# A packed-attention and MLP kernel: the next batch's first scores put right behind a weight fold, into another pair of PSUM banks, and the first residual put in front of the second scores

## The chip, the cores and the metric

The kernel runs on 1 core of a Trainium2 chip. The metric is the device time of one execution in microseconds (us). Before the change the median of 3 runs is 764.5 us (764.04 to 764.6). The engines are named as in the profile: PE is the matrix engine, PEld its weight load, DVE the vector engine, ACT the scalar engine, POOL the general engine, SP the queue that issues DMA transfers.

## The reference

Inputs are q, k, v of shape (8 batches, 8 heads, 576 tokens, 64), packs p of shape (8, 8, 32, 64), and the mixer's weights U (576 x 32), V (32 x 576), w_ch1 (512 x 2048), w_ch2 (2048 x 512). All is float32.

```python
def sm_attn(qq, kk, vv):
    s = scale * np.matmul(qq, kk.transpose(0, 1, 3, 2))
    s = s - np.max(s, axis=-1, keepdims=True)
    a = np.exp(s)
    a = a / (np.sum(a, axis=-1, keepdims=True) + 1e-09)
    return np.matmul(a, vv)
p_packed = sm_attn(p, k, v)
out = sm_attn(q, p_packed, p_packed)      # 576 tokens against 32 packs a head
# x = out with its heads side by side, (8, 576, 512)
h = x.transpose(0, 2, 1) @ U @ V
u = x + h.transpose(0, 2, 1)
result = u + np.maximum(u @ w_ch1, 0.0) @ w_ch2
```

## The kernel before, in words

The kernel never forms x. A batch's attention weights `a` (8 heads x 32 packs = 256 rows, 576 tokens) are mixed over the tokens with U and V, and u @ w_ch1 is computed as `a` times a folded weight, packs @ w_ch1. Products that need full float32 are split into a high and a low part and take three matmuls.

From batch 2 on, the program works on batch b while it prepares the attention of batch b+1 and the folded weights that come next. The order of the work is written out by hand: the string `batch_steps` is run once for each of the batches 2 to 7, and each word in it calls the next piece of one kind of work. All instructions of an engine run in the order in which the words issue them; an engine that waits at one instruction holds all behind it. What differs from batch to batch is only the tile that a word works on. In the last batch the words for the next batch's attention do nothing, so those run five times (during batches 2 to 6).

The words that this document needs, with the lines of the profile:

- **H** is half of a first-product tile (PE, L100 to L102, six matmuls of 320 or 256 columns) into one of two PSUM banks called `h_ps`, tag "k". **E** (ACT, L1034) and **L** (ACT, L801) apply the relu and empty that bank.
- **U** builds sums of such tiles (DVE, L1046, L1047, L1048), **C** splits off their high parts (ACT, L1069) and **D** their low parts (DVE, L1074). C and D write the tiles `h`.
- **G** is one turn of the second product (PE, L1085, 3 or 6 matmuls into the banks `o`). It reads what C and D wrote; the third matmul of a column's first turn is the first that reads D's part.
- **F0** folds a quarter of w_ch1 (PE, L562, into two banks `t_ps`, tag "t"; four such quarters a batch, the weights in one tile `w1s` that a DMA fills). **F1** (ACT, L574) copies the high part out, **F2** (DVE, L576) the low part, four each. F1 and F2 on one bank take turns: the third F1 waits for the first F2, the fourth for the second.
- **q0, q1, q2** transpose q (PE, L301 and L304, banks of tag "t"); q0a to q2a copy it out (L310, L312).
- **s3** makes the scores of four heads (PE, L321, into two banks); the first s3 of a batch is that of group 0, the second of group 1. **s4** transposes them out of the banks (DVE, L363, twice), **s5** takes the maximum (DVE, L367), **s6** subtracts it (POOL, L371), **s7** is the exponential (ACT, L374), **s8** the sum, the small constant and the reciprocal (DVE, L379, L381, L383; D stands between the second and the third), **s9** the product (POOL, L371), **sa** the transpose back (DVE, L387).
- **t1** transposes both groups' weights (PE, L327 and L329).
- **A** adds the residual u for half the tokens, 32 small products (PE, L1114).

PSUM has two banks of tag "t", two of tag "k" and four of `o`. A tile of a tag takes the bank that its tag's tile before last had, and waits until that is read.

The products of L562 and L321 use 64 rows and 32 columns of the PE array at a time (in the profile 64\*32), those of L1114 32 rows and 64 columns (32\*64), and all others here the whole (128\*128).

Of the kernel before, what the change touches and what calls it, by code (L numbers as in the profile page):

```python
# [20 lines left out]
def packed_attention_mixer_kernel(  # L21
# [28 lines left out]
    B, H, S, D = q.shape  # L50
    NP = p.shape[2]
    R = U.shape[1]
    DM = H * D
    DF = w1.shape[1]
    P = 128
# [15 lines left out]
    U, V, w1, w2 = (a.bitcast(I32) for a in (U, V, w1, w2))  # L71
# [37 lines left out]
    def bank():  # L109
        return psT.tile([P, 512], F32, name="t_ps", tag="t")  # L110
# [203 lines left out]
    def scores(lT, t, g, ss):  # L314

        for x in range(4):
            hs, h = slice(32 * x, 32 * x + 32), x ^ g
            for r in range(2):
                rs = slice(64 * r, 64 * r + 64)
                n = HALF[r].stop - HALF[r].start  # L320
                nc.tensor.matmul(ss[r][hs, :n], lhsT=lT[rs, g, hs], rhs=t[rs, h, :n], start=True, stop=True)  # L321
# [10 lines left out]
    def attention(b, res):  # L332

        st = {}
# [18 lines left out]
            turned(st["t", g], st["t_ps", g, h], h, scalar)  # L353

        def scores_q(g):
            ss = st["ss", g] = [bank() for _ in range(2)]
            scores(ppT[b], st["t", g], g, ss)

        def side(g, r):
# [97 lines left out]
        if b != 2:  # L457
            gh = list(product(range(2), range(2)))
            return {
                "a0": [load], "a1": [run(load_q, 1)],  # L460
                **{f"q{h}": [run(turn_q, g, h) for g in range(2)] for h in range(3)},
                **{f"q{h}a": [lambda scalar, g=g, h=h: turned_q(g, h, scalar) for g in range(2)] for h in range(3)},
                "s3": [run(scores_q, g) for g in range(2)],
                "s4": [run(side, g, r) for g, r in gh],
                "s5": [run(most, g) for g in range(2)],
                "s6": [run(each, g, "m", ALU.subtract) for g in range(2)],
                "s7": [run(power, g) for g in range(2)],
                "s8": [run(total, g, k) for g in range(2) for k in range(3)],
                "s9": [run(each, g, "s", ALU.mult) for g in range(2)],
                "sa": [run(back, g) for g in range(2)],  # L470
                "t0": [room],
                "t1": [run(tokens, k) for k in (0, 2, 4)],
                "t2": [run(split_tokens, k, False) for k in (0, 2, 4)],
                "t3": [run(split_tokens, k, True) for k in (0, 2, 4)],
                "x0": [mix1], "x1": [run(split_mix1, False)], "x2": [run(split_mix1, True)],
                "y0": [run(mix2, g, hf) for hf, g in gh],
                "y1": [run(add_mix2, g, hf) for hf, g in gh],
                "y2": [run(high_mix2, g, hf) for hf, g in gh],
                "y3": [run(low_mix2, g, hf) for hf, g in gh],
                "pu": [put],  # L480
            }
# [5 lines left out]
        def step_scores(g):  # L487
            scores_q(g)
            side(g, 0)
            side(g, 1)  # L490
# [102 lines left out]
    for z in range(2):  # L593
        a, b = (x[:, D:].rearrange("p (y z n) -> p z y n", y=2, z=2) for x in (swapped, ident))
# [665 lines left out]
    for kt in range(NK):  # L1260
# [41 lines left out]
        "Sn F2n F1n Pn Hn F1n U XO XM F1n XO F2n En F2n En XM F2n Wn Zn XO XO Yn "  # L1302
    )
    batch_steps = (
# [9 lines left out]
    )  # L1314
    joint_steps = (
# [123 lines left out]
```

## Time and profile before

| | |
|---|---|
| median of 3 runs | 764.5 us |
| the profiled execution, and its span | 765.2 us, 763.2 us |
| PE busy | 749.9 us, 98% |
| DVE, ACT, POOL busy | 587.5, 405.7, 84.9 us |
| granted TensorE clock | 1.000 |
| DMA | 151.78 MB, 199 GB/s |

In the timeline a row gives the start in us from the span's beginning, the duration of what is merged into the row, the engine, the line, what is written and read, the shape and the count; idle time before it and what ended it stand in brackets. The products of F0 and s3 stand twice in the trace. Matmuls overlap in time, so the distance between two starts says what one cost the engine, and the printed duration does not.

### The profile page before, as it was taken

To read this page: it belongs to the slowest core of one execution; us is meant where nothing else is said; L and a number is where in the kernel's file an instruction comes from. 1 tells how busy PE (TensorE), PEld (TensorE's weight loads), DVE (VectorE), ACT (ScalarE), POOL (GpSimd) and SP (SyncE) were. 2 spreads that over 40 slices of the span, in tenths; PEclk is the share of its full clock that TensorE was granted. 3 is DMA by queue.
4 is the path that set the end of the run, shared out by engine and by line. 5 is a ranking of instruction groups with operands and counts; after the bars stand their busy time and mean duration, and the time that the engine had idled before them with its cause. 6 is when DMAs were issued, how large, how long until landed. Compare 5 with 4: busy or idle time off the path is not lost.

```text
span 763.2 us, 19553 instructions
## 1 busy us (share of the span) xinstructions
PE 749.9 (98%) x7795; PEld 662.2 (87%) x7795; DVE 587.5 (77%) x1216; ACT 405.7 (53%) x1018; POOL 84.9 (11%) x116
## 2 busy tenths in 40 slices
PE   8999999999999999999999999999999999999997
PEld 6667787887878889998999989999999989999997
DVE  4799789976787768867888768867887678764876
ACT  4788765554343645555455544555554554555451
POOL 1123111010111002100201002010201020200000
PEclk9999999999999999999999999999999999999999
DMA  9999984369112874656478474657464746463672
GB/s 318 337 355 305 324 219 157 112 228 300 40 42 88 254 250 140 221 195 200 130 229 267 132 245 148 185 168 244 145 192 166 253 126 202 148 239 125 198 224 105
DMA packets 106090, 151.78 MB, mean 199 GB/s; under 512 B 40464, under 2 KB 60176, under 8 KB 102416
## 3 DMA queue, kind: packets, MB, share of 16 engines
q1 hardware_dynamic: 105856, 150.28, 61.6%
q8 instruction: 62, 1.02, 0.5%
q14 instruction: 28, 0.23, 0.1%
q10 hardware_dynamic: 144, 0.26, 0.1%
HBM read 116.56 MB, written 33.95 MB: 197 GB/s over the span
## 4 chain that ended last, share of the span: by engine, by line
PE 85%; DMA 6%; DVE 4%; ACT 3%; issue 1%; SPq 0%; POOL 0%; ACTq 0%
PE o L1085 33%; PE h_ps L100 9%; PE h_ps L101 8%; PE h_ps L102 8%; PE t_ps L562 4%; PE o L100 3%; PE o L101 3%; PE o L102 3%; DMA w1s<-w1D 2%; DMA kx<-in_k_dram 2%; PE t_ps L301 1%; PE o L1114 1%; PE s_ps L321 1%; PE t_ps L321 1%; PE m_ps L696 1%
## 5 line engine op out<-in xcount | busy, mean ns | idle before, releaser
L1085 PE MATMUL o<-w2h,h 128*128 128x256 f32 x832 | 166.9, 281 | 0.0
L100 PE MATMUL h_ps<-ah,wth 128*128 128x256 f32 (+1 forms) x512 | 157.5, 308 | 0.6 <-ACT hj L801 0.3
L101 PE MATMUL h_ps<-al,wth 128*128 128x256 f32 (+1 forms) x512 | 150.4, 294 | 0.0
L102 PE MATMUL h_ps<-ah,wtl 128*128 128x256 f32 (+1 forms) x512 | 150.3, 294 | 0.0
L1085 PEld LDWEIGHTS o<-w2h,h 128*128 128x128 f32 x832 | 136.2, 189 | 2.6 <-issue 2.6
L1074 DVE TENSOR_TENSOR h<-bits,h 128x896 fp32r<-128x896 f32 (+1 forms) x104 | 107.8, 1037 | 31.2 <-ACT h L1069 30.5
L1069 ACT CAST h<-bits 128x896 fp32r<-128x896 f32 (+1 forms) x104 | 93.7, 901 | 58.0 <-DVE bits L1048 39.7
L100 PEld LDWEIGHTS h_ps<-ah,wth 128*128 128x128 f32 x512 | 96.4, 188 | 25.2 <-ACT ppall L1034 8.4
L1085 PE MATMUL o<-w2l,h 128*128 128x256 f32 x416 | 116.0, 279 | 0.0
L101 PEld LDWEIGHTS h_ps<-al,wth 128*128 128x128 f32 x512 | 96.3, 188 | 1.0
L102 PEld LDWEIGHTS h_ps<-ah,wtl 128*128 128x128 f32 x512 | 96.3, 188 | 0.0
L1034 ACT ACTIVATE bits<-h_ps 128x256 f32<-128x256 f32 x132 | 49.5, 385 | 67.4 <-PE h_ps L102 51.5
L1085 PE MATMUL o<-tb,h 128*128 128x256 f32 x468 | 81.2, 282 | 0.1
L1085 PEld LDWEIGHTS o<-w2l,h 128*128 128x128 f32 x416 | 78.1, 188 | 0.0
L576 DVE TENSOR_TENSOR wtl<-t_ps,wth 128x256 fp32r<-128x256 f32 x128 | 49.4, 417 | 29.4 <-ACT wth L574 28.3
L1085 PEld LDWEIGHTS o<-tb,h 128*128 128x128 f32 x468 | 66.7, 189 | 0.6 <-DVE h L1074 0.3
L1046 DVE TENSOR_TENSOR bits<-bits 128x256 f32<-128x256 f32 x96 | 42.9, 447 | 28.6 <-ACT bits L1034 28.4
L574 ACT CAST wth<-t_ps 128x256 fp32r<-128x256 f32 x128 | 42.6, 376 | 27.0 <-PE t_ps L562 20.4
L452 POOL TENSOR_TENSOR al<-aT,ah 128x320 fp32r<-128x320 f32 (+1 forms) x32 | 31.4, 985 | 207.0 <-ACT ah L448 178.4
L100 PE MATMUL o<-w2h,h 128*128 128x512 f32 x128 | 52.1, 407 | 0.0
L101 PE MATMUL o<-w2l,h 128*128 128x512 f32 x128 | 50.6, 395 | 0.0
L102 PE MATMUL o<-w2h,h 128*128 128x512 f32 x128 | 50.5, 395 | 0.0
(212 smaller groups left out, 1379.8 us busy)
## 6 DMA issues: line engine op xcount, KB each, us to landing
w1s<-w1D SPq DMA_DIRECT2D x24, 1024.0 KB, 5.5
tc<-tD SPq DMA_DIRECT2D x94, 256.0 KB, 3.1
bits<-in_moe_w_ch_dram SPq DMA_DIRECT2D x32, 512.0 KB, 4.6
kx<-in_k_dram SPq DMA_DIRECT2D x16, 576.0 KB, 5.9
x<-in_q_dram SPq DMA_DIRECT2D x16, 576.0 KB, 5.9
out_dram<-os SPq DMA_DIRECT2D x33, 256.0 KB, 2.9
vt<-in_v_dram SPq DMA_DIRECT2D x32, 256.0 KB, 6.1
hD<-ppall SPq DMA_DIRECT2D x30, 256.0 KB, 4.1
```

The source lines that it names most:

```text
L100: nc.tensor.matmul(ps, lhsT=lh, rhs=rh, start=start, stop=False)
L101: nc.tensor.matmul(ps, lhsT=lh, rhs=rl, start=False, stop=False)
L102: nc.tensor.matmul(ps, lhsT=ll, rhs=rh, start=False, stop=stop)
L452: nc.gpsimd.tensor_tensor(al, aT[:, ns], ah.bitcast(F32), op=ALU.subtract)
L562: nc.tensor.matmul(f_ps[g][xs], lhsT=ppT[b][zs, g, xs], rhs=w[zs, h // 2], start=True, stop=True)
L574: nc.scalar.copy(hi[:, g], src)
L576: nc.vector.tensor_tensor(lo[:, g], src, hi[:, g].bitcast(F32), op=ALU.subtract)
L1034: nc.scalar.activation(dst[:, 256 * (i % 2):256 * (i % 2) + 256], src, AF.Relu)
L1046: vec(l[:, 4:6], s[:, 1:3], s[:, 0:1].to_broadcast([P, 2, P]), op=ALU.add)
L1069: nc.scalar.copy(h[:, ks], src)
L1074: nc.vector.tensor_tensor(lo[:, ks], src, h[:, ks].bitcast(F32), op=ALU.subtract)
L1085: nc.tensor.matmul(ps, lhsT=a, rhs=b, start=x not in self.begun, stop=last and i == 2)
```

## The change

Three things are edited. The scores of group 0 go to two banks of tag "k" instead of tag "t", for the batches 3 to 7, whose attention is prepared during the batches 2 to 6:

```diff
-            ss = st["ss", g] = [bank() for _ in range(2)]
+            ss = st["ss", g] = [(bank_k if b > 2 and g == 0 else bank)() for _ in range(2)]
```

In `batch_steps` the first s3 stands behind the fold F0 of the same stretch, with its two s4, and s5 and s6 later among the copies of that fold; two G come ahead of the H that followed the fold:

```diff
-        ... q2av D H E W s3 a1 E L Y H s4 P s4 H E s5 L C F0 U s6 E H F1 F2 F1 G F1 G F2 F1 F2 E G s7 F2 ...
+        ... q2av D H E W a1 E L Y H P H E L C E F0 s3 s4 s4 G F1 F2 U F1 s5 G F1 H F2 F1 F2 s6 E G s7 F2 ...
```

And the first A of a batch stands ahead of the second s3 (`... G E sa L E A s3 L P C G s4 ...`) instead of some ten turns later; the second A moves from ahead of an E, a U and a C to behind them, which changes no engine's order.

On ACT, POOL and SP the order of the instructions is the same before and after. On PE and DVE it changes at three places in each of the batches 2 to 6.

PE, the stretch with the fold (the pieces that follow each other in the changed kernel; `k_ps` are the scores' new banks, `tb` and `tc` operands of the second product):

```order
 L102 MATMUL h_ps<-ah,wtl 128x256
 L562 MATMUL t_ps<-w1s,ppT 32x512 x8
+L321 MATMUL k_ps<-xT,ppT 32x320
+L321 MATMUL k_ps<-xT,ppT 32x256
...
+L1085 MATMUL o<-tb_3238,h 128x256 x3
+L1085 MATMUL o<-tc,h 128x256 x3
...
+L100 MATMUL h_ps<-ah,wth 128x256
```

Before, the eight L321 stood two H earlier, and the H (L100) stood directly behind the fold, ahead of the two G (L1085). Now they stand fold, scores, G, G, H.

DVE, the same stretch, of before and then of the changed kernel, from the last D ahead of the scores to the D behind them (`e` are the scores, `m` their maximum, `s` their sum, `wtl` the folded weight's low part, `bits` the sums):

```order
L1074 TENSOR_TENSOR h<-bits,h 128x896
L363 STREAM_TRANSPOSE e<-t_ps 128x320
L363 STREAM_TRANSPOSE e<-t_ps 128x256
L367 TENSOR_REDUCE m<-e 128x18
L1046 TENSOR_TENSOR bits<-bits 128x256
L1047 TENSOR_TENSOR bits<-bits 128x128
L1048 TENSOR_TENSOR bits<-bits 128x128
L576 TENSOR_TENSOR wtl<-t_ps,wth 128x256 x4
L379 TENSOR_REDUCE s<-e 128x18
L381 TENSOR_SCALAR s<-s 128x18
L1074 TENSOR_TENSOR h<-bits,h 128x896
```

```order
L363 STREAM_TRANSPOSE e<-k_ps 128x320
L363 STREAM_TRANSPOSE e<-k_ps 128x256
L576 TENSOR_TENSOR wtl<-t_ps,wth 128x256
L1046 TENSOR_TENSOR bits<-bits 128x256
L1047 TENSOR_TENSOR bits<-bits 128x128
L1048 TENSOR_TENSOR bits<-bits 128x128
L367 TENSOR_REDUCE m<-e 128x18
L576 TENSOR_TENSOR wtl<-t_ps,wth 128x256 x3
L379 TENSOR_REDUCE s<-e 128x18
L381 TENSOR_SCALAR s<-s 128x18
L1074 TENSOR_TENSOR h<-bits,h 128x896
```

One of the four F2 (L576) and the three instructions of U now stand between the scores' transposes and their maximum. The sum (L379) and the D behind it keep their place.

PE, the second scores:

```order
 L1085 MATMUL o<-tc,h 128x256 x3
 L1085 MATMUL o<-tb_3238,h 128x256 x3
...
 L1114 MATMUL o<-ppP,aP 64x64 x32
+L321 MATMUL t_ps<-xT,ppT 32x320
+L321 MATMUL t_ps<-xT,ppT 32x256
...
+L1085 MATMUL o<-w2h_114,h 128x256
```

The scores of group 1 now follow the residual's 32 products; before they followed the two G, and the residual stood later, between two halves of the first product.

18 rows, old and new, of the table batch_steps are left out of this document.

## The prediction

> **What bounds the kernel now.** I read the page's first part, then the stretches of the batches, then the waits, then the timelines of the stretch that is changed. The timelines of the batches 3 to 6 repeat each other in this stretch, so that of batch 3 stands for four. The second line is a window of the span, its length and the busy time of PE, PEld, DVE, ACT and POOL in it.
>
> ```profile
> PE 749.9 (98%) x7795; PEld 662.2 (87%) x7795; DVE 587.5 (77%) x1216; ACT 405.7 (53%) x1018; POOL 84.9 (11%) x116
> ...
> 354.00:433.00 79.00, 79.00 (x865) 74.01 (x864) 66.70 (x141) 39.96 (x89) 9.76 (x10) 1.00 0.63 192
> ...
> PE t_ps L562 <- DMA w1s<-w1D: 1.4, 2, 0.9
> ```
>
> PE is busy for 79.00 of 79.00 us in a whole batch: nothing waits, and every microsecond taken from PE's work is a microsecond of time, as is every one in which PE is made to wait. DVE (66.70) has some slack, ACT and POOL have much. PE's only large waits on a transfer are two on w1s, one of them in the stretch that is changed, in batch 2.
>
> The timeline of PE in the stretch (start, duration of the row, count at its end):
>
> ```profile
> 355.33 0.76 PE L321 MATMUL t_ps<-xT,ppT 64*32 64x320 f32 x16
> 356.03 0.41 PE L100 MATMUL h_ps<-ah,wth 128*128 128x320 f32 x1
> ...
> 357.01 0.28 PE L100 MATMUL h_ps<-ah,wth 128*128 128x256 f32 x1
> ...
> 357.81 1.09 PE L562 MATMUL t_ps<-w1s,ppT 64*32 64x512 f32 x16
> 358.83 0.38 PE L100 MATMUL h_ps<-ah,wth 128*128 128x256 f32 x1
> ...
> 359.64 0.52 PE L1085 MATMUL o<-tb,h 128*128 128x256 f32 x3
> ...
> 360.70 0.28 PE L1085 MATMUL o<-w2h,h 128*128 128x256 f32 x1
> ...
> 362.12 1.03 PE L301 MATMUL t_ps<-ident,x 128*128 128x128 f32 x8
> ...
> 364.89 0.60 PE L1085 MATMUL o<-tb,h 128*128 128x256 f32 x3
> 365.33 0.52 PE L1085 MATMUL o<-tc,h 128*128 128x256 f32 x3
> ...
> 366.13 0.76 PE L321 MATMUL t_ps<-xT,ppT 64*32 64x320 f32 x16
> ```
>
> The blocks are scores (355.33), H1 (356.03), H2 (357.01), fold (357.81), H3 (358.83), two G (359.64), two G (360.70), q0 and q1 (362.12), and after two more H and q2 the G that I call the late one (364.89). The nine matmuls of the first two G take 1.06 us (359.64 to 360.70), 0.12 each, so the third of the late G, the first to read D's part, starts at 365.33 - 0.12 = 365.21.
>
> **What the change saves: entries and exits of small blocks.** H2 has six matmuls, the last starts at 357.01 + 5 x 0.12 = 357.60, and the fold 0.21 later instead of 0.12: an entry costs 0.09 us. H3 behind the fold takes 0.81 us (358.83 to 359.64) where six steps make 0.71: the first weights after a small block cost 0.10. Two small blocks side by side pay both once instead of twice:
>
> ```profile
> 224.21 2.07 PE L562 MATMUL t_ps<-w1t,ppT 64*32 64x512 f32 x16
> 226.21 0.41 PE L100 MATMUL h_ps<-ah,wth 128*128 128x320 f32 x1
> ...
> 325.51 0.91 PE L1114 MATMUL o<-ppP,aP 32*64 32x64 f32 x64
> 326.35 1.09 PE L562 MATMUL t_ps<-w1s,ppT 64*32 64x512 f32 x16
> 327.37 0.41 PE L100 MATMUL h_ps<-ah,wth 128*128 128x320 f32 x1
> ```
>
> At 224.21 two folds stand together (half of their records are missing) and take 2.00 us; one alone takes 1.02 (357.81 to 358.83). So the bodies hardly overlap. The same holds for residual and fold, 0.84 + 1.02. The change makes two such pairs in a batch, fold with scores and residual with scores, and saves 2 x 0.19 = 0.38 us; in five batches 1.9 us, a quarter of a percent.
>
> The Trainium skill (TensorEngine Tiling (Array Packing), Key Properties) says that a change of tiling mode drains the array and a change of tile alone does not. By it the fold and the scores, both 64\*32, need no drain between them; the two folds at 224.21, also of one mode, do not show such an overlap. What it would make of the time is the fourth rival below.
>
> **What it makes late: the first scores' chain.** Without the block at 355.33, H1 starts at 355.33 - 0.09 = 355.24, H2 0.88 later at 356.12 (before 0.98, with the 0.10 that now falls away), the fold 0.80 later at 356.92, the scores 1.02 later at 357.94. They take 0.70 (355.33 to 356.03), so the two G start at 358.64, H3 at 358.64 + 1.06 + 0.10 = 359.80, the next two G 0.71 later at 360.51, q0 is due 1.42 later at 361.93 (0.19 earlier than before, the saving), and the late G's third matmul 3.09 later (362.12 to 365.21) at 365.02. The scores themselves are made 357.94 - 355.33 = 2.61 us later, and all their followers keep their place ahead of D. Those rows, DVE first, then POOL, then ACT:
>
> ```profile
> 356.19 0.85 DVE L363 STREAM_TRANSPOSE e<-t_ps 128x320 f32<-128x320 f32 x2 [1.05 <-PE t_ps L321]
> 357.08 0.75 DVE L367 TENSOR_REDUCE m<-e 128x18 f32<-128x576 f32 x1
> 357.75 0.42 DVE L1046 TENSOR_TENSOR bits<-bits 128x256 f32<-128x256 f32 x1
> 358.20 1.13 DVE L1047 TENSOR_TENSOR bits<-bits 128x128 f32<-128x128 f32 x1
> ...
> 359.57 0.75 DVE L576 TENSOR_TENSOR wtl<-t_ps,wth 128x256 fp32r<-128x256 f32 x2
> ...
> 361.62 0.75 DVE L379 TENSOR_REDUCE s<-e 128x18 f32<-128x576 f32 x1 [0.38 <-ACT e L374]
> ...
> 362.49 1.08 DVE L1074 TENSOR_TENSOR h<-bits,h 128x896 fp32r<-128x896 f32 x1
> ...
> 383.87 0.41 DVE L1046 TENSOR_TENSOR bits<-bits 128x256 f32<-128x256 f32 x1
> ...
> 384.85 0.75 DVE L1168 TENSOR_TENSOR os<-os 128x256 f32<-128x256 f32 x2
> ...
> 357.97 1.21 POOL L371 TENSOR_TENSOR e<-e,m 128x576 f32<-128x576 f32 x1 [25.83 <-DVE m L367]
> ...
> 357.21 0.39 ACT L1034 ACTIVATE bits<-h_ps 128x256 f32<-128x256 f32 x1 [1.22 <-PE h_ps L102]
> 358.43 0.40 ACT L1034 ACTIVATE ppall<-h_ps 128x256 f32<-128x256 f32 x1
> 360.89 0.69 ACT L374 ACTIVATE e<-e 128x576 f32<-128x576 f32 x1
> ```
>
> Before, D ends at 363.57, 1.64 us ahead of the matmul at 365.21. In the changed order: transposes 0.86 behind the scores' start, at 358.80; first F2 0.89 later (356.19 to 357.08) at 359.69; U 0.38 later at 360.07; s5 0.98 later (383.87 to 384.85, a U that nothing disturbs) at 361.05; s6 0.89 later (357.08 to 357.97) at 361.94, until 363.15; s7 at 363.20 (0.05 for the handover, my estimate from DVE's 361.62 behind ACT's 361.58); the sum 0.73 later at 363.93; D 0.87 later (361.62 to 362.49) at 364.80, until 365.88. The matmul goes at 365.93: **0.91 us of waiting on D**, and 0.72 later than before. Part of the wait falls earlier, at q0: its bank is free behind the third F2, at 361.05 + 0.67 + 0.75 = 362.47, against 361.93. That is no second term, since the D chain runs beside it.
>
> The new banks cost nothing by this sum, but just so: the scores need the bank that E empties behind H2. E behind H1 moves from 357.21 to 355.24 + 1.08 = 356.32, the one behind H2 stands 1.22 later and ends at 357.94, when the scores come. At the other end H3 takes the bank of the first transpose, free at 359.3, and comes at 359.80. Every 0.1 us that E is late is 0.1 us for PE; above that the bound is E's own 0.40.
>
> **The second scores.** Residual and scores side by side save 0.19: batch 3 is then 0.53 late instead of 0.72. But the scores come 0.84 later, behind the residual, so DVE's work that hangs on them is 0.72 + 0.84 = 1.56 late, while PE, which no longer has the residual between (373.89), is only 0.53 late:
>
> ```profile
> 373.89 0.91 PE L1114 MATMUL o<-ppP,aP 32*64 32x64 f32 x64
> ...
> 379.46 1.04 PE L327 MATMUL t_ps<-ident,aT 128*128 128x128 f32 x8
> ...
> 383.75 0.52 PE L1085 MATMUL o<-tb,h 128*128 128x256 f32 x3
> 384.10 0.28 PE L100 MATMUL h_ps<-ah,wth 128*128 128x256 f32 x1
> ...
> 378.17 0.77 DVE L387 STREAM_TRANSPOSE aT<-e 128x576 f32<-128x576 f32 x1
> ...
> 382.54 1.08 DVE L1074 TENSOR_TENSOR h<-bits,h 128x896 fp32r<-128x896 f32 x1
> ```
>
> The second L327 (0.11 behind the first) reads sa's result. Due at 379.57 + 0.53 = 380.10, it gets it at 378.94 + 1.56 + 0.05 = 380.55: 0.45 of waiting, 0.98 late. The D at 382.54 ends at 383.62 + 1.56 + 0.05 = 385.23 if DVE stays as late as it was; its matmul is due at 384.10 - 0.12 + 0.98 = 384.96: 0.27 more. Both are bounded below by nothing (if DVE catches up in its gaps) and above by these numbers. I take them whole, because DVE shows few gaps there. A batch costs 0.72 - 0.19 + 0.45 + 0.27 = 1.25 us, four cost 5.0.
>
> **Batch 2** has the wait on w1s in this place:
>
> ```profile
> 279.89 1.09 PE L562 MATMUL t_ps<-w1s,ppT 64*32 64x512 f32 x16 [0.92 <-DMA w1s<-w1D]
> ...
> 288.18 0.76 PE L321 MATMUL t_ps<-xT,ppT 64*32 64x320 f32 x16
> ```
>
> The fold cannot start before 279.89 however early PE comes, since SP's order is the same. Scores at 280.91, transposes 281.77, D's end 365.88 - 358.80 = 7.08 later at 288.85, the matmul at 288.90 instead of 288.18 - 0.92 = 287.26: 1.64 late. With -0.19 + 0.45 + 0.27 that is 2.2 us.
>
> **The sum.** 5.0 + 2.2 = 7.2 us. The profiled execution took 765.2 us, 2.0 more than its span, and would take 772.4; against the median of 764.5 I predict 771.7 us.
>
> **Rivals.**
> First, only the wait on D is real, and DVE catches up before sa. For it: gaps of 0.4 us on DVE would do. Against it: of this whole batch DVE is busy for 66.70 of 79.00 us, and the two waits stand where it is fullest. Then four batches cost 0.53 and batch 2 1.45: 3.6 us, 768.1.
> Second, the other side: the chain of the first scores fits. It decides at 6.17 us from the first transpose to D's end, where I count 7.08. Then each of four batches saves 0.38, and batch 2, with its matmul due at 280.91 + 0.70 + 1.16 + 0.71 + 1.42 + 3.09 = 287.99, loses 0.73 - 0.19: 1.0 us less in all, 763.5. Against it: it needs almost the whole of U out of the way.
> Third, F2 meets s6. At 358.20 L1047 took 1.13 us while POOL's s6 ran (357.97 to 359.18); an undisturbed U is through in 0.98 altogether. If the three F2 that now run beside s6 stop likewise, the third ends at about 363.15 + 0.38, q0 is 1.6 late instead of 0.54, and the matmul comes 366.65, 0.7 worse: 3.6 us in five batches, 775.3. The Trainium skill (SBUF — State Buffer, SBUF: two separate sides) describes an exclusive lock between GpSimd and vector instructions with two SBUF inputs; F2 has one of its inputs in PSUM, so by that rule it goes on. L1047, with both in SBUF, agrees.
> Fourth, scores that start inside the fold's last half. They would come up to 1.02 / 2 = 0.5 us earlier, with all behind them: 2.5 us less than my sum, 769.2, and with the second rival's fit 761.0. The two folds at 224.21 speak against it. It is what the rule of TensorEngine Tiling in the Trainium skill would let happen.
>
> **Chances.** My forecast 0.50 (770 to 774), the first rival with the fourth's slower half 0.25 (766.5 to 770), the third 0.06, the second 0.13, the fourth with the fit 0.06. A difference under 0.2%, 1.5 us, is no change for this kernel; so the second rival counts as the same. Slower 0.81, same 0.13, faster 0.06. The range 766.5 to 774.5 holds the forecast and the first rival, with the bounds of the two later waits (nothing, or whole) and some 2 us above for E and F2; what it leaves out is the second, the faster fourth and most of the third.
>
> **What would show it.** Right: PE idle before L1085 by DVE h L1074, about 0.9 us less what q0 waited, in each of five batches; the sum (L379) released by ACT L374, and L374 by POOL L371; L301 released by DVE wtl L576; L327 by DVE aT L387. Wrong: PE busy throughout, L379 not waiting, D ending well ahead of its matmul, or a fold-and-scores block shorter than 1.7 us.

## The result, and the profile after

| | before | after |
|---|---|---|
| median | 764.3 us (764.04 to 764.6, 4 runs) | 772.52 us (771.1 to 773.08, 4 runs) |
| ratio | | 1.0105, 95% interval 1.0087 to 1.0122 |
| span of the profiled execution | 763.2 us | 770.6 us |
| PE, DVE busy | 749.9, 587.5 us | 754.4, 582.5 us |

The change costs 8.2 us in the medians and 7.4 us between the two profiled executions, from which all that follows is read; 771.7 us was forecast. The granted TensorE clock is 1.000 in both. The head of the page after with the shares of the chain that ended last, then PE's largest waits (in all, times, longest):

```profile
PE 754.4 (98%) x7795; PEld 663.7 (86%) x7795; DVE 582.5 (76%) x1216; ACT 405.8 (53%) x1018; POOL 84.5 (11%) x116
...
PE 76%; DVE 13%; ACT 5%; DMA 4%; issue 2%; SPq 1%; POOL 0%; ACTq 0%; DVEq 0%
```

```profile
PE t_ps L301 <- DVE wtl L576: 1.6, 5, 0.3
PE t_ps L329 <- DVE x L412: 1.5, 4, 0.5
...
PE o L1085 <- DVE h L1074: 0.2, 1, 0.2
```

Before, DVE had 4% of that chain; now 13%. L301, the transposes of q0, waits in all five batches, as was forecast. L329 waits in four, for DVE's L412, a wait that the prediction did not name: L412 copies the low parts of the transposed weights out of a bank of tag "t", and the last transposes (L329) take that bank.

The first stretch of batch 3 (the changed kernel comes to it 2.40 us late: the same matmul, the last L102 of 256 columns ahead of this stretch, stands at 354.20 before and at 356.60 after):

```profile
359.36 1.09 PE L562 MATMUL t_ps<-w1s,ppT 64*32 64x512 f32 x16
360.24 0.92 PE L321 MATMUL k_ps<-xT,ppT 64*32 64x320 f32 x16
361.09 0.62 PE L1085 MATMUL o<-tb,h 128*128 128x256 f32 x3
...
364.75 1.19 PE L301 MATMUL t_ps<-ident,x 128*128 128x128 f32 x8 [0.32 <-DVE wtl L576]
...
367.67 0.81 PE L1085 MATMUL o<-tb,h 128*128 128x256 f32 x3
368.32 0.52 PE L1085 MATMUL o<-tc,h 128*128 128x256 f32 x3
...
361.23 0.85 DVE L363 STREAM_TRANSPOSE e<-k_ps 128x320 f32<-128x320 f32 x2 [3.68 <-PE k_ps L321]
362.00 0.39 DVE L576 TENSOR_TENSOR wtl<-t_ps,wth 128x256 fp32r<-128x256 f32 x1
...
362.75 0.29 DVE L1047 TENSOR_TENSOR bits<-bits 128x128 f32<-128x128 f32 x1
...
363.95 1.28 DVE L576 TENSOR_TENSOR wtl<-t_ps,wth 128x256 fp32r<-128x256 f32 x3
366.09 0.75 DVE L379 TENSOR_REDUCE s<-e 128x18 f32<-128x576 f32 x1 [0.86 <-ACT e L374]
...
366.96 1.08 DVE L1074 TENSOR_TENSOR h<-bits,h 128x896 fp32r<-128x896 f32 x1
...
365.37 0.69 ACT L374 ACTIVATE e<-e 128x576 f32<-128x576 f32 x1 [0.31 <-POOL e L371]
...
364.18 1.16 POOL L371 TENSOR_TENSOR e<-e,m 128x576 f32<-128x576 f32 x1 [30.04 <-DVE m L367]
```

Fold and scores take 361.09 - 359.36 = 1.73 us, the 1.02 and the 0.70 of the two alone. DVE idles 3.68 us ahead of the scores and is then late to the end of the stretch. Against the timeline before, and with the 2.40 taken off, q0 is 0.23 late (362.12 to 364.75), the late G 0.38 (364.89 to 367.67), its second three matmuls, behind the first that reads D's part, 0.59 (365.33 to 368.32). PE itself was early until then: the last matmul ahead of q0 starts at 362.00 before and at 364.16 after, which is 0.24 early with the 2.40 taken off.

What it leads to is best seen in the chain of work that ended last, here in batch 5 (start, us, what): before, every piece of it in this stretch is PE's, these two among them:

```profile
543.52 0.69 PE t_ps L321 x12
...
559.60 0.22 PE t_ps L329 x2
```

After, it leaves PE at the second scores and comes back only at L329:

```profile
548.71 0.84 PE o L1114 x53
549.55 0.81 PE t_ps L321 x12
550.36 0.83 DVE e L363 x2
...
553.20 1.14 DVE bits L1047
...
554.69 0.94 ACT h L1069
...
555.75 0.26 ACT e L374
...
556.22 0.94 ACT h L1069
...
557.19 1.09 DVE h L1074
...
560.10 1.18 DVE bits L1047
...
564.68 0.69 DVE x L412
...
565.42 0.41 PE t_ps L329 x2
```

So a batch can be cut at two DVE rows, the second L363 (called the evacuation of the second scores below) and the first L412. The rows for it, from the timelines of batch 4 and 5, first of before, then of after; each first row is batch 4's L412:

```profile
480.56 1.28 DVE L412 TENSOR_TENSOR x<-t_ps,xh 128x512 fp32r<-128x512 f32 x2
...
544.31 0.85 DVE L363 STREAM_TRANSPOSE e<-t_ps 128x320 f32<-128x320 f32 x2 [0.78 <-PE t_ps L321]
...
558.67 1.28 DVE L412 TENSOR_TENSOR x<-t_ps,xh 128x512 fp32r<-128x512 f32 x2
...
559.43 0.39 PE L329 MATMUL t_ps<-ident,aT 128*64 128x128 f32 x2
```

```profile
485.19 1.28 DVE L412 TENSOR_TENSOR x<-t_ps,xh 128x512 fp32r<-128x512 f32 x2
...
549.43 0.78 DVE L387 STREAM_TRANSPOSE aT<-e 128x576 f32<-128x576 f32 x1 [0.79 <-POOL e L371]
550.35 0.85 DVE L363 STREAM_TRANSPOSE e<-t_ps 128x320 f32<-128x320 f32 x2
...
564.68 1.28 DVE L412 TENSOR_TENSOR x<-t_ps,xh 128x512 fp32r<-128x512 f32 x2
...
565.42 0.41 PE L329 MATMUL t_ps<-ident,aT 128*64 128x128 f32 x2 [0.33 <-DVE x L412]
```

Before, from L412 to L412 it is 558.67 - 480.56 = 78.11 us: 63.75 to the evacuation of the second scores and 14.36 from there. After, 79.49: 65.16 and 14.33. Where L329 waits, it starts 0.74 behind L412 (564.68 to 565.42); before, 0.76 behind without a wait. **Before, then, PE was busy all the time, and yet from the second scores to L329 it had only 0.02 us to spare against the chain through DVE.** By these rows whatever makes that chain later costs its full length, and a saving on PE between the second scores and L329 could not show; no run takes time from PE there alone, so this last part is worked out and not shown. Ahead of the second scores it is otherwise: DVE idled 0.78 us for them before.

### The profile page after: what moved, and what is told of

Read it like the earlier page. It is cut to its first block, busy times and chain, and to the rows that moved or that the text cites. A ratio compares the mean times of both kernels' runs of the same rounds, so it can differ in the third digit from the quotient of the medians.

```text
span 770.6 us, 19539 instructions
## 1 busy us (share of the span) xinstructions
PE 754.4 (98%) x7795; PEld 663.7 (86%) x7795; DVE 582.5 (76%) x1216; ACT 405.8 (53%) x1018; POOL 84.5 (11%) x116
## 3 DMA queue, kind: packets, MB, share of 16 engines
q8 instruction: 62, 1.02, 0.5%
## 4 chain that ended last, share of the span: by engine, by line
PE 76%; DVE 13%; ACT 5%; DMA 4%; issue 2%; SPq 1%; POOL 0%; ACTq 0%; DVEq 0%
PE o L1085 26%; PE h_ps L100 8%; PE h_ps L101 7%; PE h_ps L102 7%; PE t_ps L562 4%; PE o L100 3%; PE o L101 3%; PE o L102 3%; DVE h L1074 2%; ACT h L1069 2%; DVE bits L1047 2%; PE t_ps L301 2%; PE o L1114 1%; DVE e L363 1%; PE t_ps L419 1%
## 5 line engine op out<-in xcount | busy, mean ns | idle before, releaser
L1085 PE MATMUL o<-w2h,h 128*128 128x256 f32 x832 | 167.0, 281 | 0.0
L100 PE MATMUL h_ps<-ah,wth 128*128 128x256 f32 (+1 forms) x512 | 156.7, 306 | 1.3 <-ACT aP L801 0.8
L102 PE MATMUL h_ps<-ah,wtl 128*128 128x256 f32 (+1 forms) x512 | 150.3, 293 | 0.0
L1085 PEld LDWEIGHTS o<-w2h,h 128*128 128x128 f32 x832 | 136.1, 189 | 2.6 <-issue 2.6
L1074 DVE TENSOR_TENSOR h<-bits,h 128x896 fp32r<-128x896 f32 (+1 forms) x104 | 107.8, 1037 | 30.5 <-ACT h L1069 29.9
L1069 ACT CAST h<-bits 128x896 fp32r<-128x896 f32 (+1 forms) x104 | 93.7, 901 | 65.0 <-DVE bits L1048 44.5
L1085 PE MATMUL o<-w2l,h 128*128 128x256 f32 x416 | 116.0, 279 | 0.0
L100 PEld LDWEIGHTS h_ps<-ah,wth 128*128 128x128 f32 x512 | 96.5, 188 | 19.1 <-issue 5.0
L102 PEld LDWEIGHTS h_ps<-ah,wtl 128*128 128x128 f32 x512 | 96.2, 188 | 0.0
L1085 PE MATMUL o<-tb,h 128*128 128x256 f32 x468 | 82.5, 284 | 0.2 <-DVE h L1074 0.2
L1085 PEld LDWEIGHTS o<-w2l,h 128*128 128x128 f32 x416 | 78.2, 188 | 0.0
L576 DVE TENSOR_TENSOR wtl<-t_ps,wth 128x256 fp32r<-128x256 f32 x128 | 49.7, 416 | 31.1 <-ACT wth L574 29.4
L1085 PEld LDWEIGHTS o<-tb,h 128*128 128x128 f32 x468 | 66.8, 188 | 3.9 <-issue 2.6
L100 PE MATMUL o<-w2h,h 128*128 128x512 f32 x128 | 52.1, 407 | 0.0
L102 PE MATMUL o<-w2h,h 128*128 128x512 f32 x128 | 50.5, 395 | 0.0
```

The costliest lines, as they stand in the source:

```text
L100: nc.tensor.matmul(ps, lhsT=lh, rhs=rh, start=start, stop=False)
L102: nc.tensor.matmul(ps, lhsT=ll, rhs=rh, start=False, stop=stop)
L576: nc.vector.tensor_tensor(lo[:, g], src, hi[:, g].bitcast(F32), op=ALU.subtract)
L1069: nc.scalar.copy(h[:, ks], src)
L1074: nc.vector.tensor_tensor(lo[:, ks], src, h[:, ks].bitcast(F32), op=ALU.subtract)
L1085: nc.tensor.matmul(ps, lhsT=a, rhs=b, start=x not in self.begun, stop=last and i == 2)
```

## The experiments

Each kernel is compared with runs of the kernel before in the same session, whose medians were 765.7 us (for the first four kernels below the changed one), 765.5 (for the next four) and 766.0 us (for the last four); the changed kernel was measured beside 764.3. Medians of different sessions are therefore compared by their ratios. In the words of the order, `A` is the residual, `s3` the scores, `s5` the maximum, `s7` the exponential, `s8` sum and reciprocal.

| kernel | median, us | ratio to before (95%) | L412 to L412, batch 4 to 5 | of it to second L363 | from there | first L412 | four periods | last L412 to end |
|---|---|---|---|---|---|---|---|---|
| before | 764.3 | | 78.11 | 63.75 | 14.36 | 303.50 | 333.56 | 122.05 |
| changed | 772.5 | 1.0105 (1.0087 to 1.0122) | 79.49 | 65.16 | 14.33 | 305.64 | 338.82 | 122.02 |
| scores only | 774.1 | 1.0106 (1.0086 to 1.0126) | 79.49 | 65.15 | 14.34 | 305.47 | 339.61 | 122.72 |
| residual only | 768.3 | 1.0032 (1.0021 to 1.0042) | 78.93 | 64.60 | 14.33 | 303.89 | 336.61 | 122.16 |
| maximum first | 769.8 | 1.0050 (1.0032 to 1.0069) | 78.75 | 64.42 | 14.33 | 306.47 | 335.87 | 123.53 |
| residual behind | 773.8 | 1.0107 (1.0076 to 1.0138) | 79.30 | 64.97 | 14.33 | 304.87 | 338.35 | 124.92 |
| both of these | 770.5 | 1.0069 (1.0055 to 1.0082) | 78.74 | 64.40 | 14.34 | 304.59 | 335.95 | 123.69 |
| before, residual behind | 768.8 | 1.0047 (1.0033 to 1.0060) | 78.69 | 63.64 | 15.05 | 304.01 | 336.58 | 122.08 |
| reciprocal early | 775.4 | 1.0136 (1.0116 to 1.0155) | 79.75 | 64.70 | 15.05 | 305.75 | 339.61 | 122.80 |
| before, second scores early | 769.4 | 1.0050 (1.0037 to 1.0063) | 78.64 | 62.97 | 15.67 | 303.83 | 337.16 | 122.80 |
| maximum first, residual old | 770.6 | 1.0062 (1.0045 to 1.0080) | 78.75 | 64.41 | 14.34 | 305.29 | 335.62 | 123.04 |
| residual behind the product | 766.2 | 1.0008 (0.9995 to 1.0021) | 78.10 | 63.75 | 14.35 | 303.06 | 333.57 | 121.54 |
| residual ahead of the product | 769.5 | 1.0048 (1.0033 to 1.0062) | 78.90 | 63.58 | 15.32 | 304.10 | 336.67 | 121.58 |
| sum late | 768.9 | 1.0036 (1.0021 to 1.0050) | 78.40 | 64.07 | 14.33 | 304.35 | 334.12 | 122.55 |

The distances are taken from the same three rows of each kernel's timeline. The last three columns add up to the start of the last matmul: batch 2's first L412, four periods (batch 3 to 6) and the rest. The first of them also holds what the program's head did in that execution: the last L412 ahead of batch 2 stands at 229.62 before, at 229.64 in the changed kernel and up to 2.0 us later in the others. So kernels are compared by the four periods.

**Scores only.**

```diff
-E sa L E A s3 L ... D E N H R ... U E U C A F0n
+E sa L E s3 L ... D E A N H R ... U A E U C F0n
```

> The change with both first residuals back at their old places, so only the scores' move and their banks are left. Theory (two separate late chains): the waits around q0 and the late G stay as in the changed kernel (net +0.58 us a batch there against before), and the waits on DVE further on (H's bank behind L801, L329 behind L412, about 0.195 + 0.09 + 0.49 = 0.78 a batch) vanish, while the 0.19 that the residual's block saves is given back. Over four batches about 4 x 0.58, with some 2 us of batch 2, less what the fold's wait on its weights swallows before batch 4: 767 to 769 us. Rival (the residual in front of the second scores is harmless, all is the scores' move): 772 to 773, with L329 still waiting on DVE L412.

Against its own session's kernel before it is as slow as the whole change (1.0106 and 1.0105). The theory fell; the rival had the time right and its sign wrong. L329 no longer waits, yet the batch is as long as with the whole change (79.49), and the four periods 0.8 longer. The evacuation of the second scores is as late as in the changed kernel (65.15), and only the place where PE meets that lateness is another: H, for a bank behind L801, in place of L329.

```profile
555.16 0.94 ACT L1069 CAST h<-bits 128x896 fp32r<-128x896 f32 x1 [1.42 <-DVE bits L1048]
556.00 0.22 ACT L801 ACTIVATE aP<-h_ps 128x64 f32<-128x64 f32 x1
...
556.27 0.42 PE L100 MATMUL h_ps<-ah,wth 128*128 128x320 f32 x1 [0.48 <-ACT aP L801]
```

ACT stood 1.42 us for DVE's U, with L801 queued behind it. A wait's name says where the lateness came out, not where it came from.

**Residual only.** The kernel before with `A` moved as in the change.

```diff
-E sa L E s3 L ... D E A N H R ... U A E U C F0n
+E sa L E A s3 L ... D E N H R ... U E U C A F0n
```

> The kernel before with only the first residuals moved as in the change (the first one in front of the second scores). Theory: the residual's own block of small matmuls disappears into its neighbours' (0.19 us a batch saved), but DVE's second-scores work starts about 0.65 to 0.84 us later against TensorE, so that H waits on L801 or L329 on L412 for 0.3 to 0.6 us a batch: 764.5 to 766.5 us. Rival (the second-half waits exist only because the first half has already made DVE late): no such waits, 763.3 to 764.

This is 2.6 us above its session's kernel before, where 0.2 to 2.2 was expected: a little more, and the waits that the rival denied are there (L329 for L412). The evacuation is 0.85 late (64.60 against 63.75), the period 0.82. The 0.19 us of a block saved is nowhere to be seen in the time. The two parts of the change lose 6.05 and 3.05 us in the four periods, together 5.26: they do not add, since one evacuation waits for both.

**Maximum first.**

```diff
-E F0 s3 s4 s4 G F1 F2 U F1 s5 G F1 H F2 F1 F2 s6 E G s7 F2 P
+E F0 s3 s4 s4 s5 G F1 F2 F1 s6 G F1 H F2 F1 F2 E G s7 F2 U P
```

> The change with the order of DVE's first stretch turned round: the scores' maximum directly behind their evacuation, then the four fold adds, then U. POOL's and ACT's part of the softmax can start some 1.3 us sooner. Theory (the chain scores, maximum, POOL, exp, reciprocal, D is what holds q0 and the late G): the hold on DVE D goes and q0's goes or shrinks to below 0.2; about 0.5 us a batch for four batches, 770 us or, if the slack also takes in the later waits, down to 767. If U, now late, holds C and so the late G, the wait appears at L1085 with C in front of it and the time stays at 772. Rival (the hold is the price of the block of fold and scores itself and not of any chain on DVE): 772 to 773, the gaps at q0 unchanged.

As the theory says: PE waits for neither L576 nor D there, and a batch is 0.74 shorter than with the change (78.75 against 79.49). The hold was the chain's, not the price of the merged block. What is left, 0.64 over the period before, is an evacuation 0.67 late. In the profiled execution 1.5 of the 2.95 us that the four periods gain is lost again near the end, where DVE waits 0.92 us longer for a reload of hidden rows. This kernel's row, and the changed kernel's:

```profile
719.02 0.42 DVE L1046 TENSOR_TENSOR bits<-bits 128x256 f32<-128x256 f32 x1 [1.28 <-DMA bits<-hD]
```

```profile
720.16 0.43 DVE L1046 TENSOR_TENSOR bits<-bits 128x256 f32<-128x256 f32 x1 [0.36 <-DMA bits<-hD]
```

Why the reload lands later in some executions was not tried and stays open; in the last column it is worth up to 2.9 us.

**Residual behind.** The changed kernel with `A` behind the second `s3`.

```diff
-E sa L E A s3 L
+E sa L E s3 A L
```

> The change with the first residual directly behind the second scores in place of directly in front of them: the same merged block on TensorE, the scores 0.84 us sooner for DVE. Theory (the residual in front makes DVE late, and that is where the second half's holds come from): the holds at H (0.195), L327 (0.09) and L329 (0.49) vanish, 0.78 a batch over four batches, 3.1 us: about 769.4 us (768.6 to 770). Rival (DVE is late there because the first half left it late, whichever stands first): 772 to 773 with L329 still waiting on DVE L412.

773.8 us, 1.0107: the expectation fell, the rival held. The second scores start 0.99 sooner behind the last L412 (63.30 against 64.29), but the evacuation only 0.19 (64.97 against 65.16): DVE's own transpose back of the first group, behind POOL, ends then and no sooner.

```profile
548.43 0.78 DVE L387 STREAM_TRANSPOSE aT<-e 128x576 f32<-128x576 f32 x1 [0.79 <-POOL e L371]
549.32 0.85 DVE L363 STREAM_TRANSPOSE e<-t_ps 128x320 f32<-128x320 f32 x2
```

The changed kernel thus has two late paths into one instruction, less than 0.2 us apart. To take away one shows nearly nothing. All the kernels here fit this: in batch 5 the evacuation starts 0.86 us behind the start of the second scores or 0.10 behind the end of the first group's L387, whichever is later, within 0.03 us in thirteen of the fourteen (in "reciprocal early" the second scores were themselves held up half way).

**Both of these.** Maximum first, and the residual behind the scores.

> The maximum first (as in the run before it) and the first residual behind the second scores. In every run so far a batch's extra time equals, within 0.03 us, how late DVE starts the second scores' evacuation (second L363) against TensorE: 1.42 late and 1.39 lost with the change, 1.21 and 1.19 with the residual behind, 0.68 and 0.65 with the maximum first, 0.85 and 0.82 with the residual alone. Theory: behind that instruction DVE has no slack as far as its L412, and two things release it, the scores themselves and DVE's own turn back of the first group (L387), which waits for POOL. With the maximum first the turn back ends only 0.14 us ahead of the evacuation, so scores that come 0.84 earlier start it only 0.06 to 0.1 earlier: 0.55 to 0.62 a batch, about 0.3 us less in all than with the maximum first alone, near 769.5 us. Rival (the residual's place alone decides once the first stretch fits): 0.65 x 4 less, 767 us.

A period of 78.74 against 78.75: the rival fell, and of the 0.3 us in all that the theory promised nothing shows. The ratio (1.0069) is no better than with the maximum first alone (1.0050).

**Before, residual behind.**

```diff
-E sa L E s3 L ... D E A N H R
+E sa L E s3 A L ... D E N H R
```

> The kernel before with nothing but the first residual put directly behind the second scores, so that one block of small matmuls takes the place of two. Theory (DVE without slack from the second L363 to its L412): the evacuation starts no sooner, TensorE's saving of about 0.19 us a batch lies behind it and comes back as a wait of the same size for DVE L412 or ACT L801: within 0.3 us of the kernel before. Rival (TensorE is the bound there and the block's saving counts): 5 x 0.19, about 0.9 us faster than the kernel before.

Both readings fell: 768.8 us, 0.58 a period lost, though the evacuation is not late (63.64). Here the time goes behind it, 15.05 in place of 14.36. DVE's second L1074 waits for ACT's second L1069, and that for a product of PE (the row of before first, under it this kernel's two):

```profile
551.15 1.09 DVE L1074 TENSOR_TENSOR h<-bits,h 128x896 fp32r<-128x896 f32 x1 [0.43 <-ACT h L1069]
```

```profile
553.04 0.94 ACT L1069 CAST h<-bits 128x896 fp32r<-128x896 f32 x1 [0.53 <-PE o L1085]
...
554.01 1.09 DVE L1074 TENSOR_TENSOR h<-bits,h 128x896 fp32r<-128x896 f32 x1 [0.92 <-ACT h L1069]
```

C writes a tile `h` that a G still reads. The residual ahead of that G makes it end later: a second cause, which the first had covered.

**Reciprocal early.**

```diff
-s8 q0 s8 D q1 q0a H N H s8 q1av s9 q2
+s8 q0 s8 s8 s9 D q1 q0a H N H q1av q2
```

> As with the maximum first and the residual behind, and DVE's reciprocal (L383) ahead of D (L1074) instead of behind it, so that POOL's division and the turn back L387 come about 0.9 to 1.1 us sooner; D comes 0.27 later. Theory (L387 of the first group is what then starts DVE's second stretch late): the evacuation is released by the second scores again, at most 0.1 late or even 0.19 early against TensorE, and batches 3 to 6 cost 0 to 0.1 each more than before, with only batch 2 left: 766 to 767.5 us. If D's 0.27 holds the late G, TensorE waits there for DVE L1074 by up to 0.2 a batch. Rival (DVE's load and not its order costs the time): no better than the maximum first alone, 769 to 770.

775.4 us, the worst of all (1.0136); the theory fell. POOL's division did start 1.2 us sooner, and met DVE's L1168, which works in SBUF alone:

```profile
546.61 1.03 DVE L1074 TENSOR_TENSOR h<-bits,h 128x896 fp32r<-128x896 f32 x1
547.55 1.38 DVE L1168 TENSOR_TENSOR os<-os 128x256 f32<-128x256 f32 x1
```

```profile
546.84 1.81 POOL L371 TENSOR_TENSOR e<-e,s 128x576 f32<-128x576 f32 x1 [2.58 <-DVE s L383]
```

L1168 took 1.38 us where it takes 0.42, the division 1.81 where it takes 1.16. The transpose back came no sooner, and the residual ahead of the product added its 0.7.

**Before, second scores early.** The kernel before with the second scores and the residual 0.7 us sooner.

```diff
-H N H s8 q1av s9 q2 G q2a G E sa L E s3 L ... D E A N H R
+H N q2 H s8 q1av s9 G q2a s3 A G E sa L E L ... D E N H R
```

> The kernel before with the last pair of transposes of the second query one half-product earlier, the second scores two thirds of a product (0.7 us) earlier and the first residual directly behind them. If the evacuation's start is what counts, DVE may start it 0.4 to 0.7 us sooner (its turn back L387 ends 0.78 ahead of it), and now the block's 0.19 can show: 5 x 0.19 and perhaps a little of DVE's waits, 0.9 us faster than the kernel before. If the transposes' bank or the copy L312 is not free in time, TensorE waits 0.2 to 0.4 a batch there, and the time is 1 to 2 us above.

The evacuation does come 0.78 sooner (62.97), and 1.31 is lost behind it (15.67), L329 waiting for L412: the residual's second cause outweighs it. The expectation fell, since it was written without that cause.

**Maximum first, residual old**: both causes taken away as far as an order can.

```diff
-E sa L E A s3 L ... D E N H R
+E sa L E s3 L ... D E A N H R
```

> The change with the maximum first and both first residuals at their old places. The theory of one cause (DVE late at the second L363) has fallen: with the residual behind the second scores in the kernel before, that evacuation was not late at all, and 0.6 to 0.8 us a batch were lost all the same. Theory now, two causes: (a) the first group's chain through POOL to DVE L387 starts DVE's second stretch late; (b) the residual moved in front of the products pushes the product that frees the tile h 0.66 later, ACT's second L1069 waits for it, DVE L1074 behind that, and all of DVE as far as L412. With the maximum first, (a) leaves the evacuation 0.65 late, of which DVE's idle 0.43 in front of the second L1074 takes most; with the residual at its old place (b) is gone. So 0 to 0.25 us a batch in batches 4 to 6 between one batch and the next against 0.65 with the maximum first alone, and no wait of L329 for L412. The whole time still has batch 2 and a wait near the end for a reload of hidden rows: 766.5 to 768.5 us. Rival (only the lateness of the evacuation counts): 0.62 a batch, as with the maximum first.

770.6 us: the theory fell, the rival held. L329 waits once in place of four times, H waits for L801 instead, and the second part is 14.34. But the period stays at 78.75, 0.64 above before: the evacuation is 0.66 late, and none of that was taken up by DVE's idle 0.43. ACT's exponential and second L1069 stand in that gap, and they hang from DVE's own U (554.69 to 557.19 in the chain above). Idle time that one's own lateness moves along is no slack.

**Residual behind, and ahead of, the product that frees the tile.** Two kernels, the residual moved forward in the kernel before, and one product between them.

```diff
-s7 D S G W H C G L L D E A N H R
+s7 D S G W A H C G L L D E N H R
```

```diff
-s7 D S G W H C G L L D E A N H R
+s7 D S A G W H C G L L D E N H R
```

> The kernel before with the first residual moved only so far forward that it stands directly behind the product that frees the tile h. Theory (b): that product ends when it did, ACT's L1069 and DVE's L1074 start when they did, nothing is lost and nothing won: 0 us a batch, no wait of L329. Rival (any residual in front of that half of the first product makes h_ps, and so DVE, late): 0.3 to 0.8 a batch.

> The same, but the residual directly in front of the product that frees the tile h, one product earlier. Theory (b): that product ends 0.8 us later, the second L1069 of ACT starts about 0.6 later and is released by TensorE, and DVE's chain carries it to L412: 0.5 to 0.8 us a batch, L329 waiting 0.3 to 0.5 for DVE L412, about 3 us in all. Rival (the place against that product means nothing): the same time as with the residual behind the product.

766.2 and 769.5 us; periods 78.10 and 78.90; L329 waits in none and in four batches. Both rivals fell. The second cause is shown, with its rows in the second kernel:

```profile
553.14 0.94 ACT L1069 CAST h<-bits 128x896 fp32r<-128x896 f32 x1 [0.87 <-PE o L1085]
...
554.12 1.09 DVE L1074 TENSOR_TENSOR h<-bits,h 128x896 fp32r<-128x896 f32 x1 [1.41 <-ACT h L1069]
```

**Sum late.** As maximum first with the residual old, the reciprocal right behind D, and DVE's sum L1168 (word N) out of POOL's way.

```diff
-D q1 q0a H N H s8 q1av s9 q2 ... s7 D S G W H C
+D s8 s9 q1 q0a H H q1av q2 ... s7 D N S G W H C
```

> As the maximum first with the residuals at their old places, and DVE's reciprocal L383 directly behind the first L1074, its sum L1168 moved from there to between the next two L1074, where DVE idled 0.43. POOL's division starts 0.33 sooner and has DVE's copy out of PSUM (L310) beside it instead of L1168, which an earlier POOL division had stretched from 0.42 to 1.38 us. The turn back L387 and the evacuation start 0.3 to 0.4 sooner: 0 to 0.2 us a batch less than in the run with L1168 in its place; if the stretched L1168 only moved its harm elsewhere, no gain.

The evacuation comes 0.34 sooner (64.07), the period is 78.40, the four periods together within 0.6 us of before: the best version with the scores moved. It still loses 0.36%; in the profiled execution 0.85 us lie ahead of the first L412 and 0.5 behind the last. No version beat the kernel before; the residual behind the product (1.0008, 0.9995 to 1.0021) is level with it.

## Why the prediction was right in time, and where its steps were wrong

**Batch 2 and the later batches.** Forecast 2.2 us and four times 1.25, 7.2 in all. Measured by the rows of L412: 2.14 at the first, then 1.66, 0.83, 1.38 and 1.39, 7.40 in all. The 0.83 is a batch like the last two less 0.57: before, the fold ahead of batch 4 waited for w1s and started 0.77 behind the last matmul (445.44 to 446.21); in the changed kernel PE comes later and the fold starts 0.20 behind (449.18 to 449.38):

```profile
446.21 1.09 PE L562 MATMUL t_ps<-w1s,ppT 64*32 64x512 f32 x16 [0.49 <-DMA w1s<-w1D]
```

The prediction left that cushion out; it measured 0.57 us. Why batch 3 lost 1.66 is open; the kernel before was 0.27 quicker there (77.84) than from batch 4 to 5 (78.11). That 7.40 lies so near the forecast's 7.2 is therefore luck in part: a normal batch costs more than 1.25, and batch 4 less.

**The blocks.** Fold and scores 1.73 us: the bodies do not overlap, the fourth rival is false. By the rule of the Trainium skill (TensorEngine Tiling (Array Packing), Key Properties) two blocks of one mode need no drain between them. The trace agrees: next to the two alone, 0.01 us is left for anything between them. It shows no overlap of the bodies either. The new banks cost nothing there, as forecast.

**"Every microsecond taken from PE's work is a microsecond of time".** This step is wrong. PE was busy throughout, but between the second scores and L329 the chain through DVE was as long to 0.02 us. The saving of 0.38 us a batch that was counted on it did not reach the time. Its first half is there on PE (0.24 early ahead of q0) and is lost at once in q0's wait; even with the maximum first and the residual at its old place, where the second scores start 0.15 sooner behind L412 than before (62.74 against 62.89), the period is 0.64 longer. Of the second half, "residual and scores side by side save 0.19", no run shows the worth by itself: with the residual beside the scores in the kernel before, the four periods are 3.02 us longer, and that is the price of the residual's new place.

**The first scores' chain.** Forecast 7.08 us from the first transpose to D's end; measured 361.23 to 368.04, 6.81: the transposes passed on 0.12 sooner, the first F2 and POOL's subtraction 0.07 each, and U took the 0.98 that was forecast. More than the 6.17 available: the second rival is false. Of the "0.91 us of waiting on D" the prediction put a part at q0, 0.54 by its times, which leaves 0.37 at D. Measured: q0, due 0.19 early, came 0.23 late, so it was held 0.42; the late G was held about 0.2 (367.67 to 368.32 is 0.65, before 364.89 to 365.33 is 0.44). The matmul behind D was 0.59 late in place of 0.72. This step was right in kind and 0.13 too large.

**Third rival.** The F2 beside s6 took 1.28 us for three; they did not stop. The first rival is false as well: the late waits are real.

**"DVE's work that hangs on them is 0.72 + 0.84 = 1.56 late".** Right in kind: 1.41 was measured (65.16 against 63.75). Mis-addressed in what follows. The prediction made of it 0.45 at L327 and 0.27 at the D behind it. In batch 3 L327 was held 0.1 and that D not at all; L329, which no term named, was held 0.49, H before it 0.2 (by L801 in ACT's queue). The sum, 0.78 against 0.72, was near because DVE's lateness was near, not because the places were. The experiments say more than these places: the lateness had two paths into one L363 (first group's transpose back, residual ahead of the scores), so that taking either away gains 0.2 us or nothing.

**The residual in front of products** was costed at nothing but its order against the scores. It has a price of its own, 0.6 to 0.8 us a batch in the two kernels that show it alone (0.58 and 0.79), through the tile `h`. In the changed kernel this stayed hidden, since there the evacuation was later still.

## What to carry to other kernels

A busy engine is not the only bound. Where, over the same stretch, a chain through a second engine is as long, a delay on that chain shows whole, and a saving on the first engine in that stretch need not show at all. Cut a repeating stage at one instruction of each engine and compare the distances; an edit's cost then stands in one of them, whatever name the wait has. Of a block that is moved forward, ask also which products it pushes back and who waits to overwrite what these read.

## What the runs showed of the hardware

DVE and POOL, where both worked in SBUF, stopped each other. With the reciprocal early, POOL's division started 0.23 us behind the start of an L1074 (546.84 against 546.61) and took 1.81 us in place of 1.16; the L1168 behind that L1074 took 1.38 in place of 0.42. This fits a division that runs from L1074's end (547.64) for its 1.16 us to 548.80, nearly the 548.65 of its row, and an L1168 that runs only after it. The three F2 beside POOL's s6, with one operand in PSUM, ran on (1.28 us for three). The Trainium skill (SBUF — State Buffer, SBUF: two separate sides) describes this as a lock that the first of the two holds for its whole instruction, for a DVE operation with two SBUF inputs. The trace agrees for the division. L1168 ends at 548.93; by that rule it would start at the division's end, 548.65 by its row, and end 0.42 later at 549.07, so it came 0.14 sooner (0.29 sooner if the division ends at 548.80).

The same shows in the chain that sets the batch. Two L1047 in it, 1.14 and 1.18 us at 553.20 and 560.10 where an undisturbed one takes 0.29, stand beside POOL in the changed kernel as they do in the kernel before:

```profile
552.97 1.21 POOL L371 TENSOR_TENSOR e<-e,m 128x576 f32<-128x576 f32 x1 [3.58 <-DVE m L367]
...
559.96 1.16 POOL L371 TENSOR_TENSOR e<-e,s 128x576 f32<-128x576 f32 x1 [5.17 <-DVE s L383]
```

That is 1.7 of the 14.33 us behind the second evacuation. To move these two apart was not tried; it is where DVE's chain, and with it some slack for any change of this kind, could come from.
